# Keeping the tiles of placed sink values over the batches and filling them piece by piece in an attention and feed-forward kernel

## The chip, the cores and the metric

The kernel runs on one core of a Trainium2 chip. The core has a matrix engine (TensorE, PE in the profile; its weight loads are PEld), a vector engine (VectorE, DVE), a scalar engine (ScalarE, ACT), a general one (GpSimd, POOL) and SyncE (SP), which issues most of the DMAs here. Each engine works through a queue of its own; semaphores order the engines among each other. The metric is the time of one execution on the device in microseconds, over several runs.

## The reference

Attention over a sliding window with a few sink keys that every query may see, and then a dense feed-forward layer with softplus:

```python
batch, n_heads, seq, head_dim = (4, 8, 768, 64)
n_sink, window = (4, 128)

scores = scale * np.matmul(q, k.transpose(0, 1, 3, 2))
is_sink = pos[None, :] < int(n_sink)
rel = pos[:, None] - pos[None, :]
in_window = (rel >= 0) & (rel < int(window))
scores = np.where(is_sink | in_window, scores, -1000000000.0)
a = np.exp(scores - np.max(scores, axis=-1, keepdims=True))
a = a / (np.sum(a, axis=-1, keepdims=True) + 1e-09)
attn_out = np.matmul(a, v)

x = attn_out.transpose(0, 2, 1, 3).reshape(B * S, H * D)   # 3072 x 512
h = x @ w_in                                               # 512 x 2048
g = np.maximum(h, 0.0) + np.log1p(np.exp(-np.abs(h)))
out = g @ w_out                                            # 2048 x 512
```

## The kernel before

**Tiles and stages.** The 768 positions of a batch are cut into three chunks of 256 queries, so there are twelve chunks over four batches. A chunk has eight heads, and the steady loop of `_fast` (line 637) takes one head of attention per step: step i works at head i mod 8 of chunk i div 8. Beside it, the same step runs one of eight slices of the feed-forward layer of the chunk before (`up`, `softplus`, `gate`, `residue`, `down`). The first 17 steps are written out by hand in `START`, since the weights are loaded and split there; from step 17 on, each step goes through the letters "JjGL" and then those of `STEADY` (line 845). Step numbers below are those of this loop; e stands for i mod 8.

**Numbers in two parts.** TensorE multiplies in a reduced format here, so every operand is split into a high part, rounded to that format, and a low part, the rest. Products are then formed from high by high, high by low and low by high. The first two chunks (`EXACT` is 2) go without that split.

**Order.** Inside `_fast` the order of every engine is the order in which the program issues the instructions. The queue of an engine is therefore the letters' order, and an instruction early in a step stands ahead of all that the same engine does later in it.

**What one step does for a head** (the names are those of the methods of `_Attention`):

- `weights_t` (letter W) turns the normalised weights by TensorE into PSUM; ScalarE or VectorE copies the high part to `th` (line 48 or 50), VectorE subtracts it to get the low part `tl` (line 56). POOL then masks both with four `affine_select` instructions (lines 308 and 311) into `pt`.
- `values` (V) multiplies: first the sink part (line 327, which reads the placed sink values `vs`), then the window part (line 333, which reads `pt`).
- `normalise` (N) works four heads ahead: two products on POOL, mostly (line 264). `out` (O) adds the two halves of the result; on odd heads POOL forms the low part `xl` (line 56).
- `split` (p) prepares the scores of a later head: VectorE subtracts in lines 56, `qkh` and `kl`. `residue` (R) subtracts `gl` on VectorE.
- In even steps VectorE also does two reductions (line 440) over the split weights, until those are all checked.

**The sinks.** The first eight keys of a batch are held apart as sinks. For a group of four heads g (0 or 1), line 327 multiplies by a tile `vs` of 128 rows, four heads and 128 columns. Its first 64 rows hold the eight sink values of each head on a row of their own, zero elsewhere, the high part in columns 0 to 63 and the low part in columns 64 to 127. The other 64 rows are zero.

It is filled on POOL by `sinks(g)`: letter J, two steps ahead of a chunk, for g = 0, and letter j, three steps ahead of the fifth head, for g = 1. Both stand first in their step. This happens at the first chunk of each batch and at chunk 2, the first that is split; chunks 0 and 1 have small tiles `vsf` of their own. In the steady loop, J comes at the head of steps 22, 46 and 70 (e = 6) and j at the head of steps 17, 25, 49 and 73 (e = 1).

For g = 0 the load of the raw values (`load_sinks`, line 137, SyncE's queue) comes first, then on POOL: the high part `vsh` (line 151), the low part in place (line 152), the zero fill of the 64 rows (line 60), and a placement of each part (line 159). For g = 1 it is the fill and the two placements. Each batch takes a new tile from a pool with one buffer, so the first writer waits until TensorE has read the old one.

Of the kernel before, what the change touches and what calls it, by code (L numbers as in the profile page):

```python
# [11 lines left out]
F32 = mybir.dt.float32  # L12
F32R = mybir.dt.float32r
# [5 lines left out]
ALU = mybir.AluOpType  # L19

B, H, S, D = 4, 8, 768, 64
DM, DFF = 512, 2048
P = 128
# [4 lines left out]
CT = CH * P  # L28
# [9 lines left out]
G = 4  # L38
# [20 lines left out]
def _zero(nc, out, finite):  # L59
    nc.gpsimd.tensor_scalar(out, finite, 0.0, 0.0, ALU.mult, ALU.add)  # L60


def _turn(engines, k):

    return engines[min(k, len(engines) - 1)]
# [57 lines left out]
class _Attention:  # L123
# [16 lines left out]
    def sinks(self, g):  # L140

        c, nc, b = self.c, self.c.nc, self.b
        raw = c.vsr[b]
        if self.exact:
            c.vs[b, g] = c.lp.tile([P, G, D], F32, tag=f"vsf{g}", name=f"vsf{g}", bufs=1)
            nc.gpsimd.memset(c.vs[b, g][:], 0.0)
            self._place(c.vs[b, g][:32], raw[:32, g : g + 1], 32)
            return
        if g == 0:
            c.vsh[b] = c.lp.tile([64, 2, D], F32R, tag="vsh", name=f"vsh{b}", bufs=1)  # L150
            nc.gpsimd.tensor_scalar(c.vsh[b][:], raw[:], 1.0, 0.0, ALU.mult, ALU.add)
            nc.gpsimd.tensor_tensor(raw[:], raw[:], c.vsh[b][:], ALU.subtract)
        c.vs[b, g] = c.lp.tile([P, G, P], F32R, tag=f"vs{g}", name=f"vs{b}_{g}", bufs=1)
        _zero(nc, c.vs[b, g][64:].rearrange("p (a e) d -> p a (e d)", a=2), c.sk[64:].bitcast(F32).unsqueeze(1).broadcast_to([64, 2, CT]))
        for src, o in ((c.vsh[b], 0), (raw, D)):
            self._place(c.vs[b, g][:64, :, o : o + D], src[:, g : g + 1], 64)

    def _place(self, out, src, rows):
        self.c.nc.gpsimd.tensor_tensor(  # L159
# [198 lines left out]
def _weight_dma(c, s, k, half):  # L358

    src = c.a["w"][s, k, :, half * WH : (half + 1) * WH]
    tag = f"{WTAG[k]}{s}{half}"
    r = c.wp.tile([P, 4 * WH if c.w64 else 2 * WH], I16 if c.w64 else F32, tag=tag, name=f"{tag}r")
    if c.w64:
        c.nc.sync.dma_start(r[:, : 4 * WH - 1], src.bitcast(I16)[:, 1:])
    else:
        c.nc.sync.dma_start(r[:, :WH], src)  # L370
    c.raw[s, k, half] = r
# [7 lines left out]
def _weight_top(c, e, eng):  # L379

    if not c.w64:
        return
    up = c.top[e] = c.upper[c.turn]
    c.turn ^= 1
    _copy(c.nc, eng, up[:].bitcast(F16)[:, 1::2], _weight_words(c.raw[e])[1])
# [25 lines left out]
def _weight_high(c, e, eng):  # L415

    s, k, half = e
    n = (4, 2)[k]
    tag = f"{WTAG[k]}{s}{half}"
    c.w[e] = c.wp.tile([P, 2, n // 2, WC // n], F32R, tag=tag, name=tag)  # L420
    w, x = _weight_parts(c, e)
    _copy(c.nc, eng, w[:, 0], x)


def _weight_low(c, e, eng):
    w, x = _weight_parts(c, e)
    _sub(c.nc, eng, w[:, 1], x, w[:, 0])
# [82 lines left out]
def _fast(c):  # L510

    n = c.nchunks
    att = [_Attention(c, k) for k in range(n)]
    moe = [_Moe(c, k) for k in range(n)]
    lag = 2

    def call(lst, name, every=1, *args):
        def run(i):
            k, e = divmod(i, H)
            if 0 <= i < n * H and e % every == 0:
                getattr(lst[k], name)(e // every, *args)

        return run

    blocks = sorted(((s, k) for s in range(FP) for k in range(2)), key=lambda p: p[0] + lag * p[1])
    halves = [(*b, e) for b in blocks for e in range(2)]  # L530
    checks, dmas = list(halves), list(halves)
    todo = {e: list(enumerate(halves)) for e in "acdl"}

    def dma(i):
        if dmas:
            _weight_dma(c, *dmas.pop(0))

    def engine(engines, o):
        e = _turn(engines, o)
        return "A" if e == "P" and _turn(c.WM, o) == "p" else e  # L540

    def stage(kind):
        def run(i):
            if not todo[kind]:
                return
            o, e = todo[kind][0]
            before = "acdl"["acdl".index(kind) - 1]
            while kind != "a" and todo[before] and todo[before][0][0] <= o:
                stage(before)(i)
            home = _turn(c.WM, o)  # L550
            if kind == "a":
                while any(u is c.upper[c.turn] for u in c.top.values()):
                    stage("c")(i)
            elif kind == "c" and home == "p":
                while sum(_turn(c.WM, k) == "p" for k, _ in todo["l"] if k < o) > 1:
                    stage("l")(i)
            todo[kind].pop(0)
            if kind == "a":
                _weight_top(c, e, _turn(c.WT, o))
            elif kind == "c":  # L560
                _weight_f32(c, e, home)
            elif kind == "d":
                _weight_high(c, e, engine(c.WH, o))
            else:
                _weight_low(c, e, _turn(c.WL, o) if home == "s" else "V")

        return run

    def dense(name, k, *args):
        def run(i):  # L570
            m, s = divmod(i, H)
            if 0 <= i < n * H:
                while any(e[:2] == (s, k) for _, e in todo["l"]):
                    stage("l")(i)
                getattr(moe[m], name)(s, *args)

        return run

    def sinks(g):
        def run(i):  # L580
            k = (i - g * G) // H
            if (i - g * G) % H == 0 and k < n and (att[k].first or k == c.EXACT):
                if g == 0 and k:
                    att[k].load_sinks()
                att[k].sinks(g)

        return run

    def fill(n):

        for _ in range(n):
            c.nc.tensor.matmul(c.word_ps[0][:, :CT].bitcast(F32), c.sk[:, :P], c.sk[:], start=True, stop=True)

    parts = {
        "S": (call(att, "scores"), G),
        "T": (call(att, "softmax"), G),
        "N": (call(att, "normalise"), G),
        "p": (call(att, "split"), G + 1),
        "q": (call(att, "split_v", 2), 1),
        "W": (call(att, "weights_t"), 0),  # L600
        "k": (call(att, "sink_weights", G), 0),
        "K": (call(att, "sink", G), 0),
        "V": (call(att, "values"), 0),
        "O": (call(att, "out"), 0),
        "U": (dense("up", 0), -H),
        "F": (call(moe, "softplus"), -H),
        "P": (call(moe, "gate"), -H),
        "R": (call(moe, "residue"), -H - 1),
        "D": (dense("down", 1, 0), -H - lag),
        "E": (dense("down", 1, 1), -H - lag),  # L610
        "G": (call(att, "load_v", 2), 2),
        "L": (call(att, "load"), G + 2),
        "J": (sinks(0), 2),
        "j": (sinks(1), G - 1),
        "w": (dma, 0),
        "z": (fill, 0),
        **{kind: (stage(kind), 0) for kind in "acdl"},
    }

    with c.tc.manual_schedule():  # L620
        c.word_ps = [c.ps_acc.tile([P, WH], I32, tag=f"acc{e}", name=f"word_ps{e}") for e in range(2)]
        fill(16)
        for h in (0, 2):
            att[0].load(h)
        _constants(c)
        att[0].load_v(0)
        att[0].load_sinks()
        att[0].load(4)
        att[0].load_v(1)
        att[0].load(6)  # L630
        c.turn = 0
        c.upper = [c.lp.tile([P, WH], I32, tag=f"vs{e}", name=f"upper{e}", bufs=1) for e in range(2)]
        for t in c.upper:
            c.nc.gpsimd.memset(t[:], 0)
        for part in c.START.split():
            parts[part[0]][0](int(part[1:] or 0))
        for i in range(2 * H + 1, (n + 1) * H + lag + 1):
            for part in "JjGL" + c.STEADY[i % H == 0]:
                run, ahead = parts[part]
                run(i + ahead)  # L640
            if i >= 2 * H + lag and i % 2 == 0 and checks:
                _weight_check(c, *checks.pop(0))
            if i == n * H + lag:
                for e in checks:
                    _weight_check(c, *e)
                _fast_signs(c)
            if i == n * H + 2 * lag:
                _fast_flag(c)
# [154 lines left out]
def _kernel(tc, a, out):  # L803
    nc = tc.nc
    c = Ctx()
    c.nc, c.tc, c.a, c.out = nc, tc, a, out
    c.E = dict(qkh="A", ql="V", kl="V", vh="A", vl="P", xh="A", xl="P", gl="V", out="AV")
    c.x, c.vs, c.vsr, c.vsh = {}, {}, {}, {}
    c.w64 = a["w"].dtype == mybir.dt.int64
    nc.scalar.preload_act_table_set("natural_log_exp_and_others")  # L810
    with ExitStack() as keep:
# [99 lines left out]
```

## Time and profile before

| | us |
|---|---|
| runs: median (lowest, highest) | 728.58 (728.37, 729.44), 3 runs |
| profiled execution, first to last instruction (span) | 728.3 |
| mean granted clock of TensorE, share of full | 0.998 |
| VectorE busy | 580.1 (80%) |
| GpSimd busy | 380.2 (52%) |
| GpSimd, line 159, placements of `vs` x16 | 5.7 + 5.6 |
| GpSimd, line 60, zero fills of `vs` x8 | 5.2 |
| GpSimd, line 152, low parts x4 | 2.8 |
| GpSimd, line 151, high parts x4 | 1.6 |

The span is that of the one execution which the profiler recorded; the median of the runs lies 0.3 us above it. A busy engine is not by itself a bound: what counts is where TensorE, which is busy nearly all the time, stands idle, and which engine's instruction ended that idle time. The timeline shows this in brackets behind a row. Rows of one operation that follow each other directly are merged into one, with their count at its end.

### The profile page before, as it was taken

To read this page: it belongs to the slowest core of one execution; us is meant where nothing else is said; L and a number is where in the kernel's file an instruction comes from. 1 tells how busy PE (TensorE), PEld (TensorE's weight loads), DVE (VectorE), ACT (ScalarE), POOL (GpSimd) and SP (SyncE) were. 2 spreads that over 40 slices of the span, in tenths; PEclk is the share of its full clock that TensorE was granted. 3 is DMA by queue.
4 is the path that set the end of the run, shared out by engine and by line. 5 is a ranking of instruction groups with operands and counts; after the bars stand their busy time and mean duration, and the time that the engine had idled before them with its cause. 6 is when DMAs were issued, how large, how long until landed. Compare 5 with 4: busy or idle time off the path is not lost.

```text
span 728.3 us, 13881 instructions
## 1 busy us (share of the span) xinstructions
PE 701.0 (96%) x4535; PEld 623.7 (86%) x4535; DVE 580.1 (80%) x1693; ACT 452.1 (62%) x1104; POOL 380.2 (52%) x682
## 2 busy tenths in 40 slices
PE   6889999999999999999999999999999999999995
PEld 5577789988998998988999899898898898999994
DVE  6899988878988988887888887987888888855341
ACT  4689847656666665756666666665665766653431
POOL 5867476565555564565544554565555465452000
PEclk9999999999999999999999999999999999999999
DMA  9876613121221311411321322222221312100000
GB/s 311 302 294 209 196 49 95 52 70 57 81 71 45 108 49 50 120 52 46 100 67 49 98 63 63 78 77 59 78 67 57 96 49 78 59 12 1 30 1 33
DMA packets 40875, 63.21 MB, mean 87 GB/s; under 512 B 4634, under 2 KB 22362, under 8 KB 40794
## 3 DMA queue, kind: packets, MB, share of 16 engines
q1 hardware_dynamic: 40506, 61.97, 27.4%
q8 instruction: 38, 0.62, 0.4%
q14 instruction: 43, 0.35, 0.2%
q10 hardware_dynamic: 288, 0.26, 0.1%
HBM read 55.93 MB, written 6.29 MB: 85 GB/s over the span
## 4 chain that ended last, share of the span: by engine, by line
PE 70%; DVE 10%; ACT 7%; POOL 7%; issue 4%; DMA 1%; POOLq 0%; ACTq 0%
PE h L459 29%; PE acc L498 9%; PE acc L496 9%; PE acc L497 9%; PE x L333 5%; PE t L297 2%; POOL pt L308 2%; PE s L230 2%; PE s L231 2%; POOL pt L311 2%; ACT mt L466 1%; PE x L327 1%; ACT a L250 1%; ACT mt L467 1%; POOL vs L159 1%
## 5 line engine op out<-in xcount | busy, mean ns | idle before, releaser
L459 PE MATMUL h<-xh,wi 128*128 128x256 f32 x1536 | 253.6, 287 | 0.0
L459 PEld LDWEIGHTS h<-xh,wi 128*128 128x128 f32 x1536 | 211.0, 191 | 1.6 <-issue 0.5
L264 POOL TENSOR_SCALAR a<-a,rc 128x128 f32<-128x128 f32 x178 | 69.8, 405 | 185.1 <-DVE rc L257 150.0
L459 PE MATMUL h<-xl,wi 128*128 128x256 f32 x768 | 154.5, 283 | 0.0
L496 PE MATMUL acc<-wo,gh 128*128 128x512 f32 x384 | 151.7, 395 | 0.0
L498 PE MATMUL acc<-wo,gl 128*128 128x512 f32 x384 | 150.9, 393 | 0.7 <-DVE gl L56 0.7
L497 PE MATMUL acc<-wo,gh 128*128 128x512 f32 x384 | 150.6, 392 | 0.0
L459 PEld LDWEIGHTS h<-xl,wi 128*128 128x128 f32 x768 | 119.6, 192 | 0.0
L474 DVE SCALAR_TENSOR_TENSOR mt<-h,mt 128x512 f32<-128x512 f32 x96 | 66.0, 688 | 66.9 <-ACT mt L468 58.5
L466 ACT ACTIVATE mt<-h 128x512 f32<-128x512 f32 x96 | 57.2, 595 | 96.4 <-PE h L459 96.4
L250 ACT ACTIVATE a<-a,stats 128x136 f32<-128x136 f32 x192 | 76.3, 398 | 55.7 <-DVE stats L249 55.1
L498 PEld LDWEIGHTS acc<-wo,gl 128*128 128x128 f32 x384 | 72.1, 188 | 17.7 <-DVE gl L56 1.1
L496 PEld LDWEIGHTS acc<-wo,gh 128*128 128x128 f32 x384 | 72.1, 188 | 12.8 <-issue 0.3
L497 PEld LDWEIGHTS acc<-wo,gh 128*128 128x128 f32 x384 | 72.2, 188 | 9.0
L56 DVE TENSOR_TENSOR gl<-mt,gh 128x512 fp32r<-128x512 f32 x96 | 74.6, 777 | 0.3
L308 POOL TENSOR_SCALAR_AFFINE_SELECT pt<-tl 128x256 fp32r<-128x256 f32 x80 | 60.0, 750 | 27.8 <-DVE tl L56 27.5
L308 POOL TENSOR_SCALAR_AFFINE_SELECT pt<-th 128x256 fp32r<-128x256 f32 (+1 forms) x96 | 42.6, 443 | 39.2 <-ACT th L48 35.7
L467 ACT ACTIVATE mt<-mt 128x512 f32<-128x512 f32 x96 | 60.7, 633 | 3.1
L468 ACT ACTIVATE mt<-mt 128x512 f32<-128x512 f32 x96 | 60.7, 632 | 3.1
L48 ACT CAST qkh<-qk 128x656 fp32r<-128x656 f32 x80 | 59.5, 743 | 0.0
L333 PE MATMUL x<-pt,vv 128*128 128x256 f32 (+1 forms) x216 | 48.7, 328 | 7.8 <-POOL pt L311 7.8
L56 DVE TENSOR_TENSOR kl<-qk,qkh 128x400 fp32r<-128x400 f32 x80 | 53.7, 671 | 2.5
(185 smaller groups left out, 1238.2 us busy)
## 6 DMA issues: line engine op xcount, KB each, us to landing
qk<-qk SPq DMA_DIRECT2D x160, 164.0 KB, 3.1
vr<-v SPq DMA_DIRECT2D x32, 192.0 KB, 2.7
out<-o SPq DMA_DIRECT2D x24, 256.0 KB, 2.1
vr<-v SPq DMA_DIRECT2D x16, 128.0 KB, 2.2
q<-q SPq DMA_DIRECT2D x7, 256.0 KB, 4.8
k<-k SPq DMA_DIRECT2D x8, 200.0 KB, 4.4
wi00r<-w SPq DMA_DIRECT2D x1, 511.8 KB
wi01r<-w SPq DMA_DIRECT2D x1, 511.8 KB, 6.2
```

The source lines that it names most:

```text
L56: (nc.vector if eng == "V" else nc.gpsimd).tensor_tensor(out, a, b, ALU.subtract)
L250: nc.scalar.activation(a, a, AF.Exp, bias=nm, scale=-1.0, accum_out=sm[:, j : j + 1])
L264: (nc.vector if eng == "V" else nc.gpsimd).tensor_scalar(a, a, rc[:, j : j + 1], 0.0, ALU.mult, ALU.add)
L308: nc.gpsimd.affine_select(pt[:, e, :, 1], src[:], [[0, CH], [1, P]], ALU.is_ge, 0.0, base=0, channel_multiplier=-1)
L333: nc.tensor.matmul(x[:, :, o], w, pt[:, :, m], start=False, stop=n == 2, skip_group_check=True)
L459: nc.tensor.matmul(h[:, j], wt, x, start=k == 0, stop=k >= len(prods) - 2, skip_group_check=True)
L466: nc.scalar.activation(t[:], h[:], AF.Abs)
L467: nc.scalar.activation(t[:], t[:], AF.Exp, scale=-1.0)
L474: nc.vector.scalar_tensor_tensor(t[:], h[:], 0.0, t[:], ALU.max, ALU.add)
L496: nc.tensor.matmul(acc[:], gh[:, j, q], wh, start=f == 0, stop=False, skip_group_check=True)
L497: nc.tensor.matmul(acc[:], gh[:, j, q], wl, start=False, stop=False, skip_group_check=True)
L498: nc.tensor.matmul(acc[:], gl[:, j, q], wh, start=False, stop=f == 2 * FP - 1, skip_group_check=True)
```

## The change

The tile `vs` of each group is made once, at chunk 2, kept in `c.vst[g]` and written anew for each batch. The rows of zeros are filled only then. For the three later batches the seven remaining pieces of work are spread by `next_sinks`, which stands behind the letters of a step: the load at the end of the step with e = 1 of the chunk before the batch's first, the high part at e = 2, the low part at e = 3, the two placements of group 0 at e = 4 and 5, and those of group 1 at e = 0 and 1 of the batch's first chunk. Chunk 2 is filled as before.

```diff
         if g == 0:
-            c.vsh[b] = c.lp.tile([64, 2, D], F32R, tag="vsh", name=f"vsh{b}", bufs=1)
-            nc.gpsimd.tensor_scalar(c.vsh[b][:], raw[:], 1.0, 0.0, ALU.mult, ALU.add)
-            nc.gpsimd.tensor_tensor(raw[:], raw[:], c.vsh[b][:], ALU.subtract)
-        c.vs[b, g] = c.lp.tile([P, G, P], F32R, tag=f"vs{g}", name=f"vs{b}_{g}", bufs=1)
-        _zero(nc, c.vs[b, g][64:].rearrange("p (a e) d -> p a (e d)", a=2), c.sk[64:].bitcast(F32).unsqueeze(1).broadcast_to([64, 2, CT]))
-        for src, o in ((c.vsh[b], 0), (raw, D)):
-            self._place(c.vs[b, g][:64, :, o : o + D], src[:, g : g + 1], 64)
+            self.sinks_high()
+            self.sinks_low()
+        vs = c.vst[g] = c.lp.tile([P, G, P], F32R, tag=f"vs{g}", name=f"vs{g}", bufs=1)
+        _zero(nc, vs[64:].rearrange("p (a e) d -> p a (e d)", a=2), c.sk[64:].bitcast(F32).unsqueeze(1).broadcast_to([64, 2, CT]))
+        for part in range(2):
+            self.sinks_place(g, part)
+
+    def sinks_high(self):
+        c, nc, b = self.c, self.c.nc, self.b
+        c.vsh[b] = c.lp.tile([64, 2, D], F32R, tag="vsh", name=f"vsh{b}", bufs=1)
+        nc.gpsimd.tensor_scalar(c.vsh[b][:], c.vsr[b][:], 1.0, 0.0, ALU.mult, ALU.add)
+
+    def sinks_low(self):
+        raw = self.c.vsr[self.b]
+        self.c.nc.gpsimd.tensor_tensor(raw[:], raw[:], self.c.vsh[self.b][:], ALU.subtract)
+
+    def sinks_place(self, g, part):
+
+        c, b = self.c, self.b
+        c.vs[b, g] = c.vst[g]
+        src = (c.vsh, c.vsr)[part][b]
+        self._place(c.vst[g][:64, :, part * D : part * D + D], src[:, g : g + 1], 64)
...
-            if (i - g * G) % H == 0 and k < n and (att[k].first or k == c.EXACT):
+            if (i - g * G) % H == 0 and k < n and (k == 0 or k == c.EXACT):
...
+    def next_sinks(i):
+
+        k, e = divmod(i + H, H)
+        if k <= c.EXACT or k > n:
+            return
+        if k < n and att[k].first and 0 < e < 6:
+            a = att[k]
+            if e < 4:
+                (a.load_sinks, a.sinks_high, a.sinks_low)[e - 1]()
+            else:
+                a.sinks_place(0, e - 4)
+        elif att[k - 1].first and k - 1 > c.EXACT and e < 2:
+            att[k - 1].sinks_place(1, e)
...
             for part in "JjGL" + c.STEADY[i % H == 0]:
                 run, ahead = parts[part]
                 run(i + ahead)
+            next_sinks(i)
```

More of the change, by code (lines that the diff above doesn't have):

```diff
@@ L807, in _kernel @@
     c.E = dict(qkh="A", ql="V", kl="V", vh="A", vl="P", xh="A", xl="P", gl="V", out="AV")
-    c.x, c.vs, c.vsr, c.vsh = {}, {}, {}, {}
+    c.x, c.vs, c.vst, c.vsr, c.vsh = {}, {}, {}, {}, {}
     c.w64 = a["w"].dtype == mybir.dt.int64
```

## The prediction, made before the change was run

> **What bounds the kernel now.** I write V46 for `values(46)`, W46 for `weights_t(46)`, both of step 46; the step within a chunk is e = i mod 8. Read first the page's busy time by engine: TensorE leads, and GpSimd (POOL), which alone fills sink tiles, is busy half the time.
>
> ```profile
> PE 701.0 (96%) x4535; PEld 623.7 (86%) x4535; DVE 580.1 (80%) x1693; ACT 452.1 (62%) x1104; POOL 380.2 (52%) x682
> ```
>
> So POOL work counts only where TensorE stands still for it. In a timeline each row gives start, duration, engine, line, operation and, in brackets, the idle time before it and what ended it. In TensorE's timeline after the start-up (from 85 us on) all idle stretches that are named are at L333, the first matmul that reads the masked weights `pt`. The longest come three times, at V22, V46 and V70; the fourth row below is V49.
>
> ```profile
> 153.21 0.73 PE L333 MATMUL x<-pt,vv 128*128 128x256 f32 x3 [1.57 <-POOL pt L311]
> 323.98 0.73 PE L333 MATMUL x<-pt,vv 128*128 128x256 f32 x3 [1.56 <-POOL pt L311]
> 494.74 0.73 PE L333 MATMUL x<-pt,vv 128*128 128x256 f32 x3 [1.57 <-POOL pt L311]
> 345.42 0.62 PE L333 MATMUL x<-pt,vv 128*128 128x512 f32 x2 [0.28 <-POOL pt L311]
> ```
>
> POOL's timeline before V46 says why. Its queue runs in program order; after `xl` come the five instructions of `sinks(0)`, then the selects that V46 needs.
>
> ```profile
> 318.21 0.74 POOL L56 TENSOR_TENSOR xl<-xf,xh 128x256 fp32r<-128x256 f32 x1 [0.38 <-ACT xh L48]
> 318.93 0.29 POOL L151 TENSOR_SCALAR vsh<-vsr 64x128 fp32r<-64x128 f32 x1
> 319.30 0.77 POOL L152 TENSOR_TENSOR vsr<-vsr,vsh 64x128 f32<-64x128 f32 x1
> 320.17 0.68 POOL L60 TENSOR_SCALAR vs<-sk 64x512 fp32r<-64x512 f32 x1
> 320.92 0.81 POOL L159 TENSOR_TENSOR vs<-vsh,hmask 64x256 fp32r<-64x256 f32 x1
> 321.70 0.61 POOL L159 TENSOR_TENSOR vs<-vsr,hmask 64x256 fp32r<-64x256 f32 x1
> 322.27 0.40 POOL L308 TENSOR_SCALAR_AFFINE_SELECT pt<-th 128x256 fp32r<-128x256 f32 x1
> 323.34 0.58 POOL L311 TENSOR_SCALAR_AFFINE_SELECT pt<-tl 128x256 fp32r<-128x256 f32 x1
> ```
>
> From 318.93 to 322.27, 3.34 us, the selects wait behind sinks. The last select ends at 323.92, and TensorE goes on 0.06 later.
>
> **What one stall costs.** The starts of L333 give the pace: V37, V38 and V40 in a chunk that fills no sinks, V45 and V48 in one that does.
>
> ```profile
> 258.67 0.63 PE L333 MATMUL x<-pt,vv 128*128 128x256 f32 x3
> 265.61 0.63 PE L333 MATMUL x<-pt,vv 128*128 128x256 f32 x3
> 279.69 0.63 PE L333 MATMUL x<-pt,vv 128*128 128x256 f32 x3
> 315.32 0.63 PE L333 MATMUL x<-pt,vv 128*128 128x256 f32 x3
> 338.18 0.50 PE L333 MATMUL x<-pt,vv 128*128 128x512 f32 x2
> ```
>
> V45 to V48 takes 22.86, V37 to V40 21.02: 1.84 us more. By the pace of 6.94 (265.61 - 258.67) V46 was due at 322.26 and came 1.72 late; the other 0.12 is the pipeline filling again. I charge each new stall its delay plus 0.12.
>
> **The change part by part.** Six zero fills (two a batch, three batches, 0.68 us as at 320.17) go; they were POOL time and count only inside the stall. The other pieces move to the ends of six steps, behind N and O and before the next W:
>
> - end of e=1: the load; e=2: the high part; e=3: the low part;
> - e=4 and e=5: the two placements of group 0; next chunk's e=0 and e=1: those of group 1.
>
> *The gain.* V22, V46 and V70 lose the 3.34 us. What is late next there? Step 38 is the same step without sinks:
>
> ```profile
> 262.27 0.40 POOL L308 TENSOR_SCALAR_AFFINE_SELECT pt<-th 128x256 fp32r<-128x256 f32 x1
> 262.33 0.88 DVE L56 TENSOR_TENSOR gl<-mt,gh 128x512 fp32r<-128x512 f32 x1
> 262.63 0.86 POOL L311 TENSOR_SCALAR_AFFINE_SELECT pt<-th 128x256 fp32r<-128x256 f32 x1
> 263.24 0.52 DVE L56 TENSOR_TENSOR qkh<-qk,qkh 64x256 fp32r<-64x256 f32 x1
> 263.44 0.59 POOL L308 TENSOR_SCALAR_AFFINE_SELECT pt<-tl 128x256 fp32r<-128x256 f32 x1
> 263.79 0.66 DVE L56 TENSOR_TENSOR kl<-qk,qkh 128x400 fp32r<-128x400 f32 x1
> 263.99 0.74 POOL L311 TENSOR_SCALAR_AFFINE_SELECT pt<-tl 128x256 fp32r<-128x256 f32 x1
> ```
>
> The selects end at 264.73, 0.88 ahead of V38. One placement (0.61 to 0.81) now stands before them: 0.07 to 0.27 is left, at least the handover of 0.06. The stall is gone: 3 x 1.84 = 5.52 us.
>
> *The low part, before W44* (and W20, W68):
>
> ```profile
> 306.66 0.74 POOL L311 TENSOR_SCALAR_AFFINE_SELECT pt<-tl 128x256 fp32r<-128x256 f32 x1
> 308.38 0.63 PE L333 MATMUL x<-pt,vv 128*128 128x256 f32 x3
> ```
>
> There is 0.98 between the end and V44; the piece takes up to 0.77 (319.30). Nothing is lost; the margin is 0.15.
>
> *Pieces at the ends of even steps* (high part, first placement of each group; no `xl` is due there) fall where the selects of `tl` wait for VectorE anyway:
>
> ```profile
> 312.57 0.80 POOL L308 TENSOR_SCALAR_AFFINE_SELECT pt<-tl 128x256 fp32r<-128x256 f32 x1 [0.64 <-DVE tl L56]
> 344.13 0.80 POOL L308 TENSOR_SCALAR_AFFINE_SELECT pt<-tl 128x256 fp32r<-128x256 f32 x1 [1.29 <-DVE tl L56]
> ```
>
> Before W45 POOL had 0.64 to spare, about a placement, and V45 (315.32) starts 2.75 after the first of the two `tl` selects. Before W49 1.29 was left although the three instructions of `sinks(1)` stood there: V49's 0.28 isn't the sinks', and stays. If the cover failed, a placement would cost at most 0.81 + 0.12 there; if V49's stall went too, each batch would gain 0.28 + 0.12.
>
> *The second placement of group 1, before W50* (W26, W74), is where I see a price:
>
> ```profile
> 349.27 0.75 POOL L56 TENSOR_TENSOR xl<-xf,xh 128x256 fp32r<-128x256 f32 x1 [0.39 <-ACT xh L48]
> 350.15 0.41 POOL L308 TENSOR_SCALAR_AFFINE_SELECT pt<-th 128x256 fp32r<-128x256 f32 x1
> 350.52 0.83 DVE L56 TENSOR_TENSOR gl<-mt,gh 128x512 fp32r<-128x512 f32 x1
> 351.57 0.47 POOL L311 TENSOR_SCALAR_AFFINE_SELECT pt<-tl 128x128 fp32r<-128x128 f32 x1
> 352.35 0.51 PE L333 MATMUL x<-pt,vv 128*128 128x512 f32 x2
> ```
>
> The selects end at 352.04, 0.31 ahead of V50. A placement from 350.02 ends at 350.63, after `gl` wants to start; selects and subtractions then take turns as in step 38, where the rest from 262.67 (first select done) to 264.73 took 2.06 for `gl`, `qkh`, `kl` and three selects. Here it is four selects, two of them half as long: about the same 2.06. So 352.69, TensorE at 352.75, 0.40 late, price 0.52. Bounds: nothing; or a slow placement and a select that loses a turn, 0.9 late, price 1.02. I take 0.52, the one built from step 38.
>
> *The load* moves from the head of e=6 to the end of e=1, behind the output stores on SyncE's queue:
>
> ```profile
> 291.62 0.84 SPq L507 DMA_DIRECT2D out<-o  x2
> 296.83 0.73 POOL L264 TENSOR_SCALAR a<-a,rc 128x128 f32<-128x128 f32 x2 [2.77 <-DVE rc L257]
> vr<-v SPq DMA_DIRECT2D x32, 192.0 KB, 2.7
> ```
>
> Issued at 292.46, it is wanted by the high part at 297.5, after those two products: 5 us, against 2.7 for a `vr` load six times as big. The loads behind it on that queue go later by one issue, less than the 0.84 of the two stores; they are asked for a step or more ahead. In step 17 it waits for the last reader of the old `vsr`, long done when the stores go. I count nothing. Placements also wait for readers of the old values (V43 and V47 for the two groups), over a step back.
>
> **The sum.** 3 x (1.84 - 0.52) = 3.96 us off the profiled span of 728.3 gives 724.3. The median of the runs, 728.58, lies 0.3 above the span: 724.6.
>
> **Rivals.**
>
> *All hidden.* W50's extra turn doesn't happen: 728.58 - 5.52 = 723.1. For it: the placement alone overruns W50 by only 0.61 - 0.13 idle - 0.25 margin = 0.23. Against it: `gl` is due inside the placement. 0.2.
>
> *Dearer collisions.* V50 0.9 late, and V46 0.25 late: 1.02 + 0.37 lost of 1.84, 3 x 0.45 = 1.35 off, 727.2. Margins of 0.07 speak for it, the turns of step 38 against. 0.13.
>
> *Nothing gained*: another wait takes V46's place, 728.6. Against: step 38 has none. 0.07.
>
> [...] 0.04.
>
> [...]
>
> **How the numbers follow.** My forecast holds 0.56. The range, 722.9 to 727.3, takes in the hidden case and the dearer one; outside are nothing gained and slower. This kernel's measurement can tell about 0.2% from no change, 1.46 us: faster is below 727.1. Faster 0.82 (forecast, hidden, half of dearer), same 0.13, slower 0.05.
>
> **What would show it.** Right: the 1.57 idle at V22, V46, V70 gone, V45 to V48 near 21.0; L60 with two instances for `vs`; a new idle of some 0.3 to 0.5 at V26, V50, V74; V49's 0.28 unchanged. Wrong: an idle at V44 or V46 (margins too thin), POOL waiting for the DMA of `vsr` before the high part, or VectorE slower around the pieces so that V49's wait grows.

## The result, and the profile after

| | before | changed |
|---|---|---|
| time, median (lowest, highest), us | 728.53 (728.37, 729.44), 4 runs | 724.17 (723.11, 724.55), 4 runs |
| ratio, 95% interval | | 0.9936 (0.9925 to 0.9948) |
| profiled execution: span, us | 728.3 | 722.7 |
| GpSimd busy, us | 380.2 | 373.8 |
| start of L333 (now L348) of V16, V95, us | 111.01, 668.11 | 111.49, 663.52 |
| from V16 to V95, us | 557.10 | 552.03 |

The change takes 4.4 us off, by the interval 3.8 to 5.5. The two profiled spans differ by 5.6, since the ends differ too: after V95 comes 60.2 us in the one and 59.2 in the other, with the same work. The stretch from V16 to V95, the steady steps, is free of that and is the measure used below; it is 5.07 us shorter. Its ends are the starts of these rows, TensorE's timeline, first of the kernel before, then of the changed one (columns as before: start, duration, engine, line, operation):

```profile
111.01 0.64 PE L333 MATMUL x<-pt,vv 128*128 128x256 f32 x3
668.11 0.63 PE L333 MATMUL x<-pt,vv 128*128 128x256 f32 x3
```

```profile
111.49 0.64 PE L348 MATMUL x<-pt,vv 128*128 128x256 f32 x3
663.52 0.63 PE L348 MATMUL x<-pt,vv 128*128 128x256 f32 x3
```

Around a change of batch, TensorE's timeline of the changed kernel has V45, V46, V48, V49, V50 and V51 here:

```profile
314.08 0.63 PE L348 MATMUL x<-pt,vv 128*128 128x256 f32 x3
321.01 0.63 PE L348 MATMUL x<-pt,vv 128*128 128x256 f32 x3
335.09 0.51 PE L348 MATMUL x<-pt,vv 128*128 128x512 f32 x2
342.30 0.63 PE L348 MATMUL x<-pt,vv 128*128 128x512 f32 x2 [0.24 <-POOL pt L326]
349.35 0.62 PE L348 MATMUL x<-pt,vv 128*128 128x512 f32 x2
356.26 0.51 PE L348 MATMUL x<-pt,vv 128*128 128x512 f32 x2
```

V46 carries no idle time any more and comes 6.93 after V45. V45 to V48 takes 21.01; it took 22.86, so 1.85 is won per batch. V49's idle is 0.24 where it was 0.28. V50 shows no idle in brackets, but V49 to V50 is 7.05 where it was 6.93, and V48 to V51 is 21.17 where it was 20.99 (359.17 - 338.18): about 0.2 a batch is given back there. The other two changes of batch agree within 0.03.

POOL's timeline before W46 and W50 of the changed kernel shows how the pieces lie:

```profile
316.97 0.74 POOL L56 TENSOR_TENSOR xl<-xf,xh 128x256 fp32r<-128x256 f32 x1 [0.39 <-ACT xh L48]
317.68 0.61 POOL L174 TENSOR_TENSOR vs<-vsr,hmask 64x256 fp32r<-64x256 f32 x1
318.24 0.40 POOL L323 TENSOR_SCALAR_AFFINE_SELECT pt<-th 128x256 fp32r<-128x256 f32 x1
318.60 0.40 POOL L326 TENSOR_SCALAR_AFFINE_SELECT pt<-th 128x256 fp32r<-128x256 f32 x1
318.96 0.40 POOL L323 TENSOR_SCALAR_AFFINE_SELECT pt<-tl 128x256 fp32r<-128x256 f32 x1
319.32 0.85 POOL L326 TENSOR_SCALAR_AFFINE_SELECT pt<-tl 128x256 fp32r<-128x256 f32 x1
...
346.85 0.61 POOL L174 TENSOR_TENSOR vs<-vsr,hmask 64x256 fp32r<-64x256 f32 x1
347.42 0.40 POOL L323 TENSOR_SCALAR_AFFINE_SELECT pt<-th 128x256 fp32r<-128x256 f32 x1
347.77 0.29 POOL L326 TENSOR_SCALAR_AFFINE_SELECT pt<-th 128x128 fp32r<-128x128 f32 x1
348.02 0.84 POOL L323 TENSOR_SCALAR_AFFINE_SELECT pt<-tl 128x256 fp32r<-128x256 f32 x1
348.83 0.47 POOL L326 TENSOR_SCALAR_AFFINE_SELECT pt<-tl 128x128 fp32r<-128x128 f32 x1
```

VectorE's timeline of the same two stretches:

```profile
317.73 2.17 DVE L56 TENSOR_TENSOR gl<-mt,gh 128x512 fp32r<-128x512 f32 x1
...
347.40 1.21 DVE L56 TENSOR_TENSOR gl<-mt,gh 128x512 fp32r<-128x512 f32 x1
```

Before W46, three selects take 0.40 each and run as if VectorE weren't there, and `gl`, which takes 0.67 to 0.69 alone (from 666.93 us on, behind POOL's last work), takes 2.17: it starts with the placement and ends 0.27 before the fourth select does, which it holds up to 0.85. In step 38 of the kernel before, they had taken turns one by one. Before W50 `gl` is passed by the two selects of `th` (1.21) and then holds up the third. Among all steady steps `gl` takes over 1.1 us in six only, these two in each of the three batches: the ones in which a placement stands before the selects and POOL goes on without a pause.

### The profile page after: what moved, and what is told of

Same layout as the page of the kernel before. It is cut to its first block, busy times and chain, and to the rows that moved or that the text cites. A ratio compares the mean times of both kernels' runs of the same rounds, so it can differ in the third digit from the quotient of the medians.

```text
span 722.7 us, 13866 instructions
## 1 busy us (share of the span) xinstructions
PE 701.4 (97%) x4535; PEld 624.5 (86%) x4535; DVE 581.5 (80%) x1693; ACT 452.5 (63%) x1104; POOL 373.8 (52%) x676
## 4 chain that ended last, share of the span: by engine, by line
PE 69%; DVE 14%; ACT 8%; issue 4%; POOL 3%; DMA 2%; SPq 0%; ACTq 0%; POOLq 0%; DVEq 0%
PE h L474 28%; PE acc L513 9%; PE acc L511 9%; PE acc L512 9%; PE x L348 5%; PE t L312 2%; PE s L245 2%; PE s L246 2%; DVE gl L56 2%; POOL pt L323 2%; ACT a L265 1%; PE x L342 1%; DVE kl L56 1%; ACT mt L482 1%; DVE mt L489 1%
## 5 line engine op out<-in xcount | busy, mean ns | idle before, releaser
L56 DVE TENSOR_TENSOR gl<-mt,gh 128x512 fp32r<-128x512 f32 x96 | 79.9, 832 | 0.3
L323 POOL TENSOR_SCALAR_AFFINE_SELECT pt<-th 128x256 fp32r<-128x256 f32 (+1 forms) x96 | 44.2, 460 | 36.1 <-ACT th L48 33.1
L56 DVE TENSOR_TENSOR tl<-t,th 128x256 f32<-128x256 f32 x80 | 33.2, 415 | 24.5 <-ACT th L48 24.1
```

The costliest lines, as they stand in the source:

```text
L56: (nc.vector if eng == "V" else nc.gpsimd).tensor_tensor(out, a, b, ALU.subtract)
L323: nc.gpsimd.affine_select(pt[:, e, :, 1], src[:], [[0, CH], [1, P]], ALU.is_ge, 0.0, base=0, channel_multiplier=-1)
```

## The experiments

What was being asked: is it the place in POOL's queue that pays, or the fills that are saved? What does the last placement cost? And what holds the idle that is left at e = 1?

**The change again**, to measure it more closely.

> The changed kernel once more. My theory: the gain is the queue in front of V22, V46 and V70 (3 x 1.84) less what the last placement costs before V26, V50 and V74 (3 x 0.2), so from the first matmul with pt of V16 to that of V95 it takes 552.0 us against 557.1 before, 5.1 less, and the time is about 723.7. A rival by which part of the 5.1 is lost again outside the steady steps, as the four runs (4.4 less) could say: 552.0 in the stretch, yet about 724.3 in the time.

Measured: 723.28 (722.99 to 724.38) against 728.39, ratio 0.9927 (0.9914 to 0.9941); V16 at 111.03, V95 at 663.16, a stretch of 552.13. The 5.1 of the stretch are found in the time; no loss elsewhere is needed, and the 4.4 of the first four runs agrees within the intervals.

**Spread, but filled each time.**

```diff
     def sinks_place(self, g, part):
 
         c, b = self.c, self.b
         c.vs[b, g] = c.vst[g]
+        if part == 0 and not self.chunk == c.EXACT:
+            _zero(c.nc, c.vst[g][64:].rearrange("p (a e) d -> p a (e d)", a=2), c.sk[64:].bitcast(F32).unsqueeze(1).broadcast_to([64, 2, CT]))
         src = (c.vsh, c.vsr)[part][b]
```

> The pieces spread as in the changed kernel, but the 64 rows of zeros filled again for each batch, in front of the first placement of each group. My theory (only the place in the queue counts): the fill falls where the selects of tl wait for VectorE anyway (0.1 idle plus 1.4 of margin before V45, 2.6 idle before W49), stretch 552.0, same time as the changed kernel within 0.3. Rival (the fill saved is what pays): 3 x 0.7 lost, stretch 554.1, 2.1 slower than the changed kernel.

Measured: 729.03, ratio 1.0009 (1.0000 to 1.0018), stretch 557.63 (110.90 to 668.53). Neither theory had this: all the gain is gone. In the second batch change 1.65 is lost between V45 and V48 (22.67 against 21.02) and 0.18 between V48 and V51 (21.36 against 21.18). In TensorE's timeline V46 stands idle again, and is followed by a shorter wait at 334.86 (0.33, for VectorE's `tl`):

```profile
323.37 0.74 PE L350 MATMUL x<-pt,vv 128*128 128x256 f32 x3 [0.85 <-POOL pt L328]
```

The selects of the step before were ready in time (1.35 ahead of V45). The delay goes by way of VectorE. POOL's timeline, from the fill at the end of e = 4 to the next products:

```profile
311.33 0.62 POOL L60 TENSOR_SCALAR vs<-sk 64x512 fp32r<-64x512 f32 x1
312.03 0.61 POOL L176 TENSOR_TENSOR vs<-vsh,hmask 64x256 fp32r<-64x256 f32 x1
312.59 0.40 POOL L325 TENSOR_SCALAR_AFFINE_SELECT pt<-th 128x256 fp32r<-128x256 f32 x1
...
313.67 0.40 POOL L328 TENSOR_SCALAR_AFFINE_SELECT pt<-tl 128x256 fp32r<-128x256 f32 x1
314.04 1.01 POOL L56 TENSOR_TENSOR vv<-vr,vv 128x384 fp32r<-128x384 f32 x1
319.02 0.72 POOL L281 TENSOR_SCALAR a<-a,rc 128x128 f32<-128x128 f32 x2 [3.96 <-DVE rc L274]
```

and VectorE's in that stretch:

```profile
312.53 3.08 DVE L56 TENSOR_TENSOR gl<-mt,gh 128x512 fp32r<-128x512 f32 x1
```

From the placement to `vv` POOL runs without a pause, and `gl`, begun at 312.53, ends at 315.61, 0.56 after `vv` does, a little less than the 0.67 to 0.69 that it takes alone. VectorE is 2.4 us late, so the row maxima, the exponentials and the reciprocal are late too. POOL waits 3.96 for the reciprocal (1.88 in the changed kernel), and everything behind that wait in its queue reaches V46 too late. In the changed kernel POOL has a pause in the same step, from 311.19 to 311.33, before the selects of `tl`:

```profile
310.79 0.40 POOL L326 TENSOR_SCALAR_AFFINE_SELECT pt<-th 128x256 fp32r<-128x256 f32 x1
311.33 0.80 POOL L323 TENSOR_SCALAR_AFFINE_SELECT pt<-tl 128x256 fp32r<-128x256 f32 x1
```

and there `gl` comes in:

```profile
311.19 0.67 DVE L56 TENSOR_TENSOR gl<-mt,gh 128x512 fp32r<-128x512 f32 x1
```

The fill had closed the pause.

**Kept, but in one block**, at the heads of e = 6 and e = 1 as before.

```diff
                 att[k].sinks(g)
+            elif (i - g * G) % H == 0 and k < n and att[k].first:
+                if g == 0:
+                    att[k].load_sinks()
+                    att[k].sinks_high()
+                    att[k].sinks_low()
+                for part in range(2):
+                    att[k].sinks_place(g, part)
...
-            next_sinks(i)
```

> The tiles kept and filled with zeros once, but the pieces in one block at the head of e = 6 and of e = 1, as before. My theory: POOL's block before W46 shrinks from 3.34 by the fill of 0.7, V46 comes 1.0 late and not 1.7, so an idle of about 0.87 at V22, V46 and V70 stays, and of the 1.84 a batch 0.7 is won: stretch 555.0, 2.1 faster than the kernel before. Rival (keeping the tiles is what pays): 552.0, as fast as the changed kernel.

Measured: 726.04, ratio 0.9965 (0.9951 to 0.9979), stretch 554.72 (111.14 to 665.86), as my theory had it. V46's idle in TensorE's timeline:

```profile
322.55 0.74 PE L348 MATMUL x<-pt,vv 128*128 128x256 f32 x3 [0.82 <-POOL pt L326]
```

0.87 was expected. So saving the fills alone is worth 2.4 us; spreading with the fills left in front of the placements is worth nothing; both together 5.0. The parts don't add.

**The last placement one step later**, at the end of e = 2.

```diff
-        elif att[k - 1].first and k - 1 > c.EXACT and e < 2:
-            att[k - 1].sinks_place(1, e)
+        elif att[k - 1].first and k - 1 > c.EXACT and e in (0, 2):
+            att[k - 1].sinks_place(1, e // 2)
```

> The changed kernel with the second placement of group 1 moved from the end of e = 1 to the end of e = 2, where W51 waits 0.85 for tl. My theory (this placement makes V26, V50 and V74 late by 0.1 and the step after by 0.1): stretch 551.4, 0.6 faster than the changed kernel. Rival (V50 is late because of VectorE's pace after V49): stretch 552.0, no difference.

Measured: 722.87, ratio 0.9924 (0.9910 to 0.9937), stretch 551.39 (110.65 to 662.04), 0.74 less than the change run beside it. The time itself can't tell the two apart; the stretch can, in all three batches. V48 and V51:

```profile
334.06 0.50 PE L348 MATMUL x<-pt,vv 128*128 128x512 f32 x2
...
355.03 0.51 PE L348 MATMUL x<-pt,vv 128*128 128x512 f32 x2
```

20.97, where the kernel before has 20.99. The 0.2 a batch comes from that placement; the last two runs show that it takes the reductions at e = 0 as well.

**Filled each time, in POOL's idle time**: right behind the selects of the step, not before the placement.

```diff
                 run, ahead = parts[part]
                 run(i + ahead)
+                if part == "p":
+                    zero_sinks(i)
             next_sinks(i)
...
+    def zero_sinks(i):
+
+        if i % H == 4:
+            k, g = i // H + 1, 0
+        elif i % H == 0:
+            k, g = i // H, 1
+        else:
+            return
+        if k < n and att[k].first and k > c.EXACT:
+            _zero(c.nc, c.vst[g][64:].rearrange("p (a e) d -> p a (e d)", a=2), c.sk[64:].bitcast(F32).unsqueeze(1).broadcast_to([64, 2, CT]))
```

> The spread pieces with the rows of zeros filled for each batch, as in the run with the fills kept, but the fill stands right after the selects of its step (e = 4, e = 0), where POOL then idles some 3 us for the reciprocal of N, and not before the placement. Theory S (the fill cost 5.5 us there because it closed POOL's pause before the selects of tl, and VectorE's gl, which shares something with POOL, was held off for a run of POOL instructions): the pause is back, gl near 0.7 to 1.0 in that step, V46 not stalled, stretch from V16 to V95 552.1, the time that of the changed kernel. Rival (each fill costs its own POOL time or a new wait on the tile wherever it stands): at least 3 x 0.7 lost, stretch 554.2 or more.

Measured: 724.43, ratio 0.9945 (0.9932 to 0.9959), stretch 552.20 (110.92 to 663.12): the changed kernel's, with the same fills that had cost 5.5 us. (The ratio of the times, 0.9945, lies above the 0.9927 of the changed kernel's repeat, but their intervals overlap; the stretch decides.) POOL's timeline, the fill and then the step in which `gl` had been shut out:

```profile
306.15 0.62 POOL L60 TENSOR_SCALAR vs<-sk 64x512 fp32r<-64x512 f32 x1
...
309.36 0.61 POOL L174 TENSOR_TENSOR vs<-vsh,hmask 64x256 fp32r<-64x256 f32 x1
...
310.83 0.80 POOL L323 TENSOR_SCALAR_AFFINE_SELECT pt<-tl 128x256 fp32r<-128x256 f32 x1
```

VectorE's:

```profile
310.68 0.67 DVE L56 TENSOR_TENSOR gl<-mt,gh 128x512 fp32r<-128x512 f32 x1
```

`gl` has its 0.67 back. Theory S holds as far as the pause goes, and the rival, that a fill costs its time wherever it stands, falls. That `gl` shares something with POOL was my guess, and no run shows it; what they show is this step's `gl` at 3.08 us where POOL runs on without a pause, and at 0.67 where it has one.

**The last placement twice.**

```diff
             att[k - 1].sinks_place(1, e)
+            if e == 1:
+                att[k - 1].sinks_place(1, e)
```

> The changed kernel, with the second placement of group 1 done twice at the end of e = 1, before W26, W50 and W74, where V waits for the last select as it is. If the selects are simply that much later: 0.57 more each, 3 x 0.57 = 1.7, stretch 553.8. If a longer run of POOL holds VectorE's gl off for longer and the turns come out differently: more than 1.7, up to 3 x 1.0, with gl well over 1.2 us in that step. If the two hide each other: under 1.

Measured: 727.29, ratio 0.9980 (0.9971 to 0.9989), stretch 555.18 (110.97 to 666.15): 3.05 more, 1.02 a batch, the upper of the three cases, but not for its reason. TensorE's, POOL's and VectorE's timelines around V50:

```profile
350.93 0.61 PE L348 MATMUL x<-pt,vv 128*128 128x512 f32 x2 [0.98 <-POOL pt L326]
```

```profile
347.41 1.70 POOL L174 TENSOR_TENSOR vs<-vsr,hmask 64x256 fp32r<-64x256 f32 x2
349.06 0.62 POOL L323 TENSOR_SCALAR_AFFINE_SELECT pt<-th 128x256 fp32r<-128x256 f32 x1
349.65 0.62 POOL L326 TENSOR_SCALAR_AFFINE_SELECT pt<-th 128x128 fp32r<-128x128 f32 x1
```

```profile
347.95 0.68 DVE L56 TENSOR_TENSOR gl<-mt,gh 128x512 fp32r<-128x512 f32 x1
```

Here `gl` isn't held off at all: it takes its turn between the two placements (1.70 for both, where one takes 0.61), and the subtractions after it come between the selects. The second placement, shown by itself below, starts 0.07 after the first has ended (347.41 + 0.61 = 348.02); the other two batches have the same pause of 0.07 to 0.08.

```profile
348.09 1.01 POOL L174 TENSOR_TENSOR vs<-vsr,hmask 64x256 fp32r<-64x256 f32 x1
```

In the changed kernel the select behind the one placement starts 0.04 before that placement ends, so POOL has no pause there. The strict turns of my prediction do occur, then; this one extra instruction, with turns, makes V50 1.0 late where 0.57 of work was added.

**The reductions kept away from e = 0.** Apart from V22, V46 and V70 in the kernel before, the idle that the two kernels show after the start-up is at e = 1 (V25, V33 and so on to V81).

```diff
-            if i >= 2 * H + lag and i % 2 == 0 and checks:
+            if i >= 2 * H + lag and i % 2 == 0 and i % H and checks:
```

> The changed kernel, without the two reductions over split weights at the steps with e = 0; the eight checks that fall away there come later, in the even steps from 82 on. Theory: the idle that is left, at e = 1 of each chunk (V25, V33, ..., V81, 0.24 to 0.52), is tl held up by those 1.26 us on VectorE; each costs 0.5 to 0.8 with the refill, so all eight about 5.5: stretch 546.6, time 717.8. Rival (ScalarE's softplus, for which VectorE waits 1.4 us just before, holds tl as well): at best half, 549.4, and an idle at e = 1 remains.

Measured: 717.70, ratio 0.9847 (0.9833 to 0.9860), stretch 545.80 (110.58 to 656.38). TensorE's timeline has no named idle after the start-up any more; V40 and V43 are here:

```profile
275.99 0.63 PE L348 MATMUL x<-pt,vv 128*128 128x256 f32 x3
...
296.79 0.63 PE L348 MATMUL x<-pt,vv 128*128 128x256 f32 x3
```

20.80 where it was 21.53 before. The theory holds; ScalarE's softplus isn't what holds `tl`. The stretch is 0.8 shorter than forecast; most of that is the 0.2 a batch before W50, which is gone too (V48 to V51 takes 20.45 here) though the placement stands where it stood.

**Both.** The last two edits that helped, in one kernel.

> The reductions moved away from e = 0 and the second placement of group 1 moved to the end of e = 2. If the two gains are of different places they add: stretch 546.6 - 0.7 = 545.9, time about 717.2. If V26 was late only because V25 was, the second brings nothing more: 546.6.

Measured: 717.24, ratio 0.9846 (0.9833 to 0.9859), stretch 545.83 (110.97 to 656.80). The later placement adds nothing: with the reductions out of the way V50 has 0.6 to spare in the run before. So the placement costs its 0.2 a batch only where those reductions have made VectorE late. These two kernels are the fastest of all, and can't be told apart.

## Why the prediction was right, and what in it was not

*The bound and the gain.* Right. POOL's queue held V22, V46 and V70; with the block gone, 1.85 us a batch is won where 1.84 was read from the pace of another chunk. No other wait took its place.

*The price before W50.* The place was right, the size not: 0.52 a batch forecast, 0.20 measured. Three times the difference is 0.96, most of the 1.1 us between the 3.96 forecast and the 5.07 found in the steady steps. The idle of 0.3 to 0.5 at V26, V50 and V74 that was to show it did not appear. The step that failed is that selects and subtractions "take turns as in step 38". Before W50 POOL passed `gl` with two selects, so three of POOL's instructions were done before `gl` cost it anything. When the placement was done twice the turns did come, and V50 was 1.0 late. POOL then had a pause of 0.07 in which `gl` could come in, and with one placement it had none; but step 38 has turns without a pause, so why they don't come with one placement stays open. I also put the price down to the placement alone: without the reductions at e = 0 it is nothing.

*The margins.* I had the selects 0.07 to 0.27 ahead of V46, and for V44 0.15 beyond the handover. Measured: the last select before V46 ends at 320.17, 0.84 ahead, again because `gl` waited and not the selects. The low part took 0.46 and not 0.77, so V44 had 0.57, the handover of 0.06 included.

*The even steps.* Right for this change: the pieces before W45 and W49 cost nothing, and V49's idle stayed, being VectorE's (the reductions; shown by the run without them). But my reason, that a pause before the selects of `tl` is free for POOL, is only half of it. That pause is also when VectorE's `gl` gets in, and the run with the fills in it lost most of its 5.5 us by that. The change is on the right side of it, with 0.14 us of pause left before the `tl` selects of W45. By my own figures next to nothing was to be left (0.64 less a placement of 0.61), so that it was enough was luck.

*The fills.* I counted them as POOL time only. Their saving is worth 0.75 a batch in the one-block order, and nothing if they are put in POOL's idle time. What decides is the place.

*The load.* Right: POOL doesn't wait for `vsr` in any of the steady steps.

*The rivals.* The first four runs, 724.17, lie nearer to my 724.6 than to the 723.1 of "all hidden". The repeat, 723.28, and the stretch, 5.07 less against 5.52 and 3.96, lie nearer to "all hidden". That the first figure came so close to mine is in part luck. The chances of a slower kernel, 0.04 and 0.05, were my estimate, and no run shows a ground for them: step 38 has turns, and the selects before V46 ended 0.84 early. Yet a large loss was near by, by one side being held off over many instructions: in the run with the fills before the placements `gl` took 3.08 us, and 1.83 was lost in the second batch change.

*The span.* I added 0.3 to the span to get the median. The timed runs of both kernels lie 1.7 above their own spans (728.39 against 726.7, 724.42 against 722.7), so the profiled execution of before, with its 728.3, was probably a long one; its own time is not on record. Since the sum was a difference, this moved nothing by more than its noise.

## What to carry to other kernels

Measure the margin of each step, from the last producer's end to the start of its consumer, in a chunk without the work and in one with it; a piece of work belongs in the step where that margin, or an idle stretch that waits for somebody else, is longest. Before filling such a pause on GpSimd, look at what VectorE does in it: a pause that seems free may be another engine's only turn (here `gl` took 0.67 us with a pause of 0.14 before the selects of `tl`, 3.08 without it). And take an edit apart before crediting a part: here keeping the tiles alone gave just under half of the gain, and spreading alone gave nothing or all of it, depending on where the fills stood.

## What the runs showed of the hardware

VectorE's subtraction `gl` (128x512) and a run of GpSimd instructions hold each other off, and not in equal shares: before W46 `gl` took 2.17 us where it takes 0.67 to 0.69 alone, and the fourth select 0.85 where the three before it took 0.40. The subtraction waited for one GpSimd instruction (step 38), for three (W50), for four (W46), and for the whole run, 3.08 us, when fills stood before the placements. Each time it ended 0.54 to 0.56 us after the last instruction that it had waited for. Which of them began first does not settle it: before W46 `gl` began 0.51 us ahead of the first select, and three selects went first. Before W50 it began 0.55 us into the placement and lost to the two selects after it; with a second placement behind the first, it began 0.54 into the first and went next, at the 0.07 us pause between the two. What settles it was not found. That it matters is shown: the same fills cost 5.5 us in one place and nothing in another.
